# The second FFN product as seven Strassen products in turn, over slices of 512 tokens, with its operand sums made one stage earlier

## The chip, the core and the metric

One core of a Trainium2 chip runs the whole program. The metric is the device time of one execution in microseconds (us). The core has TensorE (PE, matrix products into PSUM; its weight loads stand as PEld), VectorE (DVE), ScalarE (ACT), GpSimd (POOL) and SyncE (SP, which here only issues DMAs). POOL and SP issue the DMAs; 16 DMA engines carry them.

## The reference, cut to what matters

```python
x = attention(q, k, v)                  # linear attention with decay, 4 x 768 tokens, 512 wide
x = ((x @ w1) * (x @ w2)) @ w3 @ w_out  # 3072 tokens, 512 -> 1024 -> 512
h = x @ w_in                            # first FFN product,  512 -> 2048
g = h * (1 / (1 + exp(-1.702 * h)))
out = g @ w_out2                        # second FFN product, 2048 -> 512
```

Everything is float32. The kernel writes each operand of a product as a high part plus a low part (dtype float32r) and adds three products: high times high, high times low, low times high. One such triple is `mm3` (L222 to L225 of the kernel before): three TensorE instructions.

## The kernel before, in words

The program has three parts in time. Attention and the weights' preparation come first, together with the MoE product (tiles `psm` and `acc`, 512 tokens to a matmul). Then comes the first FFN product (class `Expand`, called the second stage here), and then the second FFN product (`contract`, the third stage).

`Expand` runs over 4 slices `s` of 768 tokens and, in each, over 8 "quads" `j` of 256 features. A quad is one 2 x 2 block product by Strassen's scheme in Winograd's form: seven products P1, P5, P4 (of the quad before), P6, P2, P3, P7, each two `mm3` of 384 columns, so 42 matmuls. Sums of the seven give four quarters of h: two halves of the features by two halves of the 768 tokens. ACT copies partial results out of PSUM (L472) and applies the gate (L482), DVE adds (L510 `s1` after P2, L513 `u2` after P3, L519 `u3` after P7). The four gated quarters go to DRAM (`gd`, one tensor to a slice `s`) in two stores of 384 KB to a quad (L485), out of a pool of five tiles `g`. PSUM tiles turn over: `a` has three, `e` and `c` two each. The right operands of the next slice (`operands`, L405) are made on DVE in nine steps; the table `NEXT` puts eight of them after set products of quads 4 to 7, and the ninth falls into the next slice's first quad.

`contract` goes over 24 batches: 6 groups of 512 tokens by 4 groups of the contraction. A batch loads the gated values (`gr`, L565, 1 MB), makes four operand sums on DVE (L576), splits seven operands into parts (ACT L597, DVE L599), and runs all seven Strassen products for two steps of the contraction: 84 matmuls of 256 columns. Seven PSUM tiles `m` gather over four batches. At the end of a token group, DVE and POOL add the seven up (L669 to L686), and four stores write `out`. The weights' seven left operands are made in the first part (`seven`), written to DRAM by `store_parts` (`sp`, 16 tensors, one to a step of the contraction) and fetched with 1792 KB to a tile (L456) by POOL's queue into eight fixed slots `op0` to `op7`, which the second and the third stage share.

All engines run in the order in which the code is written (manual schedule). A tile's memory comes free when its last reader is done, and a new tile waits for all tiles whose bytes it covers. Each DMA that SP issues also waits for the one that used the same of its eight semaphores before.

Of the kernel before, what the change touches and what calls it, by code (L numbers as in the profile page):

```python
# [16 lines left out]
P = 128  # L17
# [24 lines left out]
def tile_kernel(  # L42
# [29 lines left out]
    gd = [dram.tile([P, NQ, 2, 2 * TS], F32, name=f"gd{i}", tag=f"gd{i}") for i in range(NS)]  # L72
    sp = [dram.tile([P, 2, 7 * 256], F32, name=f"sp{i}", tag=f"sp{i}") for i in range(2 * NQ)]
# [46 lines left out]
    def store_parts(i, m, hi, lo):  # L120
        at = slice(0, 3 * 256) if m == 0 else slice(3 * 256, 7 * 256)
        for n, x in enumerate((hi, lo)):
            nc.sync.dma_start(sp[i - WI][:, n, at], x.bitcast(F32))
# [337 lines left out]
    class Expand:  # L461
# [22 lines left out]
        def store(self, g, s, j, f):  # L484
            nc.sync.dma_start(gd[s][:, j, f], g.rearrange("p h t -> p (h t)"))  # L485

        def fourth(self):
            a, s, j, g = self.open
            self.product(a, "P4", s, j)
            self.gated(g[:, 0], a)  # L490
            self.store(g, s, j, 1)
            self.open = None

        def quad(self, s, j, step):
            a, e, c = (self.bank(x) for x in "aec")
            g = [self.p.tile([P, 2, TS], F32, tag="g", bufs=5, name="g") for _ in range(2)]
# [14 lines left out]
            self.gated(g[0][:, 0], s1)  # L511
# [10 lines left out]
            self.open = a, s, j, g[1]  # L522

        def run(self):
# [5 lines left out]
            for s in range(NS):  # L530

                for j in range(NQ):

                    def step(at):
                        nonlocal nxt
                        more = s + 1 < NS
                        if more and (j, at) == (2, 3):
                            nxt = operands(s + 1, self.py)
                            next(nxt)
                        elif more and (j, at) in NEXT:  # L540
                            next(nxt)
                        elif s and (j, at) == (0, 0):
                            next(nxt)
                        if not more and (j, at) in OPENING:
                            OPENING[j, at](self.py, self.pf)

# [5 lines left out]
    batches = [(i, b) for i in range(NB) for b in range(NQ // 2)]  # L552
    raws2, mid, ops = {}, {}, {}

    def load_g(n, pool, queue=nc.sync, **at):
        if n >= len(batches):
            return
        i, b = batches[n]
        raw = raws2[n] = pool.tile([P, 2, 2, TB], F32, name="gr", **at)
        at = 0  # L560
        while at < TB:
            s, t0 = divmod(i * TB + at, 2 * TS)
            m = min(TB - at, 2 * TS - t0)
            for k in range(2):
                queue.dma_start(  # L565
                    raw[:, k, :, at : at + m], gd[s][:, 2 * b + k, :, t0 : t0 + m]
                )
            at += m

    def sums(n, pool, **at):  # L570
        (b11, b12), (b21, b22) = (
            [raws2[n][:, :, f, h * TU : (h + 1) * TU] for h in range(2)] for f in range(2)
        )
        t = mid[n] = pool.tile([P, 4, 2, TU], F32, name="gt", **at)
        for x, (a, b) in enumerate(((b12, b11), (b22, t[:, 0]), (b22, b12), (b21, t[:, 1]))):
            nc.vector.tensor_tensor(t[:, x], a, b, ALU.subtract)  # L576

    def operand_tiles(n, pool, tags, **at):
        ops[n] = [
            pool.tile([P, 7, 2, TU], F32R, tag=tag, name=f"o{w}", **at)  # L580
            for w, tag in zip("hl", tags)
        ]

    def parts_of(n):
        r = raws2[n]
        yield 0, 1, r[:, :, 0, :TU]
        for h in range(2):
            yield 1 + h, 2 + h, r[:, :, 1, h * TU : (h + 1) * TU]
        yield 3, 7, mid[n]

    def splits(n):
        todo = [
            (*(o[:, a] if b - a == 1 else o[:, a:b] for o in ops[n]), x)
            for a, b, x in parts_of(n)
        ]
        for h, l, x in todo:
            nc.scalar.copy(h, x)  # L597
        for h, l, x in todo:
            nc.vector.tensor_tensor(l, x, h.bitcast(F32), ALU.subtract)  # L599

    def split_piece(a, b):
        if a < 3:
            x = list(parts_of(0))[a][2]
            h, l = (o[:, a] for o in ops[0])
        else:
            x = mid[0][:, a - 3 : b - 3]
            h, l = (o[:, a:b] for o in ops[0])
        nc.vector.tensor_copy(h, x)
        nc.vector.tensor_tensor(l, x, h.bitcast(F32), ALU.subtract)

    RIGHT = dict(P1=0, P2=1, P3=2, P5=3, P6=4, P7=5, P4=6)
    OPENING = {
        (0, 3): lambda p, pf: load_g(0, p, tag="raw"),
        (1, 3): lambda p, pf: sums(0, pf, tag=f"op{SLOT[0]}"),
        (3, 0): lambda p, pf: (
            operand_tiles(0, pf, [f"op{SLOT[x]}" for x in (1, 2)]),
            split_piece(0, 1),
        ),
        (3, 3): lambda p, pf: split_piece(1, 2),
        (4, 0): lambda p, pf: split_piece(2, 3),  # L620
        (4, 1): lambda p, pf: fetch_left(NQ, left_tile(pf, SLOT[3])),
        (4, 3): lambda p, pf: split_piece(3, 5),
        (5, 0): lambda p, pf: split_piece(5, 7),
        (5, 3): lambda p, pf: load_g(1, pf, tag=f"op{SLOT[0]}"),
        (5, 1): lambda p, pf: fetch_left(NQ + 1, left_tile(pf, SLOT[4])),
        (6, 1): lambda p, pf: fetch_left(NQ + 2, left_tile(pf, SLOT[5])),
        (7, 1): lambda p, pf: load_g(2, pf, tag=f"op{SLOT[6]}"),
    }

    def contract(p, pf, ps):  # L630

        def store(t, x, i, h):
            rows = out[x * 2 * P : (x + 1) * 2 * P].rearrange("(q p) t -> p q t", p=P)
            at = i * TB + h * TU
            nc.sync.dma_start(rows[:, :, at : at + TU], t)

        m = {}
        for n, (i, b) in enumerate(batches):
            if n == 1:
                for x in (1, 2):  # L640
                    fetch_left(NQ + 4 + x, left_tile(pf, SLOT[x]))
            hi, lo = ops[n]
            if b == 0:
                m = {
                    x: ps.tile([P, 2, TU], F32, tag=x, name="m") for x in RIGHT
                }
                c11, c12, c21, c22, s5, u3, u4 = (
                    p.tile([P, 2, TU], F32, tag=x, name=x)
                    for x in ("c11", "c12", "c21", "c22", "s5", "u3", "u4")
                )  # L650
            for k in range(2):
                j = 2 * b + k
                end = j == NQ - 1
                for name in ("P1", "P5", "P6", "P2", "P7", "P3", "P4"):
                    r = RIGHT[name]
                    for q in range(2):
                        mm3(
                            m[name][:, q],
                            *left_parts(NQ + j, name, q),
                            hi[:, r, k],  # L660
                            lo[:, r, k],
                            j == 0 and q == 0,
                            end,
                        )
                    if not end:
                        continue
                    ps_m = m[name]
                    if name == "P1":
                        nc.scalar.copy(c11, ps_m)  # L669
                    if name == "P5":  # L670
                        nc.scalar.copy(s5, ps_m)
                    if name == "P6":
                        nc.vector.tensor_tensor(c12, ps_m, c11, ALU.add)
                        nc.gpsimd.tensor_tensor(u4, c12, s5, ALU.add)
                    if name == "P2":
                        nc.vector.tensor_tensor(c11, ps_m, c11, ALU.add)
                        store(c11, 0, i, 0)
                    if name == "P7":
                        nc.vector.tensor_tensor(u3, ps_m, c12, ALU.add)
                        nc.gpsimd.tensor_tensor(c22, u3, s5, ALU.add)  # L680
                        store(c22, 1, i, 1)
                    if name == "P3":
                        nc.vector.tensor_tensor(c12, ps_m, u4, ALU.add)
                        store(c12, 0, i, 1)
                    if name == "P4":
                        nc.vector.tensor_tensor(c21, ps_m, u3, ALU.add)  # L686
                        store(c21, 1, i, 0)
# [299 lines left out]
```

## Time and profile before

| | |
|---|---|
| median of 3 runs | 1027.27 us (1027.13 to 1027.66) |
| the profiled execution | 1028.51 us, of which the span from first to last instruction is 1026.7 us |
| TensorE busy | 991.8 us (97%), 6688 matmuls |
| VectorE busy | 647.6 us (63%) |
| ScalarE busy | 441.8 us (43%) |
| mean granted TensorE clock | 0.993 of full speed |
| moved by DMA | 202.79 MB |

A matmul's busy time is longer than the distance to the next one, since matmuls overlap. What an instruction costs on TensorE is therefore read from the distance between starts in the timeline. "Idle before" is the time that an engine stood still ahead of an instruction, with what released it.

### The profile page before, as it was taken

What the parts mean: (1) busy time and instruction counts of PE and PEld (TensorE: products, weight loads), DVE (VectorE), ACT (ScalarE), POOL (GpSimd) and SP (SyncE); (2) the same over time, 40 slices, a digit from 0 to 9 for tenths busy, and PEclk for the clock granted to TensorE, in tenths of its full rate; (3) what the DMA queues carried; (4) which work ended last, traced back from release to release, by engine and by line L of the source; (5) the groups of instructions that cost most, each with busy time, mean ns of one, the idle gap of its engine ahead of it and who ended that gap; (6) DMA issues with size and microseconds to landing.
All of it is one profiled execution on the core that took longest, in us unless ns stands there. A gap on an engine that the chain in (4) does not pass through costs nothing.

```text
span 1026.7 us, 16851 instructions
## 1 busy us (share of the span) xinstructions
PE 991.8 (97%) x6688; PEld 900.1 (88%) x6688; DVE 647.6 (63%) x1048; ACT 441.8 (43%) x875; POOL 46.1 (4%) x65
## 2 busy tenths in 40 slices
PE   4879999999999999999999999999999999999997
PEld 3668777888888888888889999999999999999997
DVE  4877888856767777742442362634646588687782
ACT  4767544433434434322113455555455343433431
POOL 3110000000000000000001000000001011011011
PEclk9999999999999999999999999999999999999999
DMA  8999645436676666650137925233469854344331
GB/s 310 336 400 361 239 155 177 151 125 220 230 269 201 223 238 215 219 177 16 55 131 313 372 96 181 102 132 151 150 220 416 330 165 162 110 138 142 106 123 41
DMA packets 80159, 202.79 MB, mean 198 GB/s; under 512 B 6736, under 2 KB 33488, under 8 KB 75088
## 3 DMA queue, kind: packets, MB, share of 16 engines
q1 hardware_dynamic: 73888, 146.14, 40.8%
q0 software_dynamic: 6192, 55.58, 13.8%
q8 instruction: 52, 0.85, 0.3%
q14 instruction: 27, 0.22, 0.1%
HBM read 129.34 MB, written 72.35 MB: 196 GB/s over the span
## 4 chain that ended last, share of the span: by engine, by line
PE 87%; DMA 6%; DVE 4%; issue 1%; ACT 1%; POOL 0%; DVEq 0%; ACTq 0%; POOLq 0%
PE psm L225 8%; PE psm L224 8%; PE psm L223 8%; PE m L223 8%; PE m L225 8%; PE m L224 8%; PE acc L224 4%; PE acc L223 4%; PE acc L225 4%; DMA qkv<-in_qkv_dram 4%; PE a L223 4%; PE a L224 4%; PE a L225 4%; PE e L223 2%; PE e L224 2%; PE e L225 2%
## 5 line engine op out<-in xcount | busy, mean ns | idle before, releaser
L223 PE MATMUL m<-oh,op 128*128 128x256 f32 x672 | 188.2, 280 | 0.0
L225 PE MATMUL m<-oh,op 128*128 128x256 f32 x672 | 187.6, 279 | 0.0
L224 PE MATMUL m<-ol,op 128*128 128x256 f32 x672 | 187.6, 279 | 0.0
L225 PE MATMUL psm<-xh,wl 128*128 128x512 f32 x384 | 149.5, 389 | 1.2 <-DVE wl L118 1.2
L224 PE MATMUL psm<-xl,wh 128*128 128x512 f32 x384 | 149.4, 389 | 0.0
L223 PE MATMUL psm<-xh,wh 128*128 128x512 f32 x384 | 149.4, 389 | 0.0
L225 PEld LDWEIGHTS m<-oh,op 128*128 128x128 f32 x672 | 126.4, 188 | 0.0
L223 PEld LDWEIGHTS m<-oh,op 128*128 128x128 f32 x672 | 126.3, 188 | 0.0
L224 PEld LDWEIGHTS m<-ol,op 128*128 128x128 f32 x672 | 125.8, 187 | 0.0
L819 DVE TENSOR_TENSOR tmp<-tmp,psm 128x512 f32<-128x512 f32 x48 | 32.9, 686 | 103.9 <-PE psm L225 92.9
L225 PEld LDWEIGHTS psm<-xh,wl 128*128 128x128 f32 x384 | 72.1, 188 | 16.5 <-DVE wl L118 1.6
L223 PE MATMUL a<-yh,op 128*128 128x384 f32 x256 | 85.6, 335 | 0.6 <-ACT u L472 0.6
L597 ACT CAST oh<-gr 128x512 fp32r<-128x512 f32 x69 | 38.3, 618 | 111.1 <-issue 53.4
L225 PE MATMUL a<-yh,op 128*128 128x384 f32 x256 | 85.5, 334 | 0.0
L224 PE MATMUL a<-yl,op 128*128 128x384 f32 x256 | 85.5, 334 | 0.0
L223 PEld LDWEIGHTS psm<-xh,wh 128*128 128x128 f32 x384 | 72.1, 188 | 15.0
L224 PEld LDWEIGHTS psm<-xl,wh 128*128 128x128 f32 x384 | 72.1, 188 | 14.9
L800 ACT CAST hh<-tmp 128x512 fp32r<-128x512 f32 x48 | 29.8, 621 | 124.4 <-DVE tmp L819 124.4
L223 PE MATMUL acc<-hh,wh 128*128 128x512 f32 x192 | 74.7, 389 | 0.0
L224 PE MATMUL acc<-hl,wh 128*128 128x512 f32 x192 | 74.7, 389 | 0.0
L225 PE MATMUL acc<-hh,wl 128*128 128x512 f32 x192 | 74.7, 389 | 0.0
L510 DVE TENSOR_TENSOR s<-c,s 128x384 f32<-128x384 f32 x32 | 17.8, 557 | 83.5 <-PE c L225 79.3
(106 smaller groups left out, 1899.7 us busy)
## 6 DMA issues: line engine op xcount, KB each, us to landing
op<-sp POOLq DMA_DIRECT2D x16, 1792.0 KB, 10.6
gd<-g SPq DMA_DIRECT2D x64, 384.0 KB, 2.5
qkv<-in_qkv_dram POOLq DMA_DIRECT2D x23, 1024.0 KB, 8.2
raw<-in_w_dram SPq DMA_DIRECT2D x32, 512.0 KB, 4.7
gr<-gd SPq DMA_DIRECT2D x30, 512.0 KB, 4.7
raw<-in_wo_dram SPq DMA_DIRECT2D x24, 512.0 KB, 5.7
raw<-in_wi_dram SPq DMA_DIRECT2D x16, 512.0 KB, 4.6
sp<-wqh SPq DMA_DIRECT2D x16, 512.0 KB, 3.4
```

Source lines behind the costliest of these rows:

```text
L223: nc.tensor.matmul(ps, wh, xh, start=start, stop=False, skip_group_check=True)
L224: nc.tensor.matmul(ps, wh, xl, start=False, stop=False, skip_group_check=True)
L225: nc.tensor.matmul(ps, wl, xh, start=False, stop=stop, skip_group_check=True)
L510: nc.vector.tensor_tensor(s1, c, s1, ALU.add)
L597: nc.scalar.copy(h, x)
L800: nc.scalar.copy(hi, t)
L819: nc.vector.tensor_tensor(t, t, pb, ALU.mult)
```

## The change

The third stage no longer walks over the contraction with all seven products at once. It takes the seven products in turn (P1, P2, P6, P5, P3, P7, P4), and for each the three slices of 512 token columns: 21 turns. A Strassen half has 4 x 384 = 1536 token columns now (the halves are those of `Expand`), and a turn is the whole contraction of one product for 512 of them: 2 row blocks x 8 steps x 3 = 48 matmuls of 512 columns. The turn's right operand is loaded ready-summed from `gd` (two halves `l0`, `l1`, 1 MB each, three tiles each), ACT copies the high part (128x2048), DVE subtracts to leave the low part in place. The left operands of one product (all 8 steps, two parts) are loaded by product from `sw`. Results that later products need stay in SBUF (`u`, in slot 7 and later slots 2 and 3), and an output is stored as soon as its last product is there.

The operand sums move into `Expand`: four subtractions of 128x384 to a quad on DVE (one after L524, three in `fourth`). A quad now stores seven operands in one DMA of 1344 KB, and its tile `g` has two buffers where there were five tiles of two quarters. In the last slice, the loads and splits of turn 0 take the place of the first batch's. `store_parts` writes the last eight weight tiles to `sw` in pieces of 256 elements. POOL's DMA scratch is halved to 8192 bytes.

```diff
-    gd = [dram.tile([P, NQ, 2, 2 * TS], F32, name=f"gd{i}", tag=f"gd{i}") for i in range(NS)]
-    sp = [dram.tile([P, 2, 7 * 256], F32, name=f"sp{i}", tag=f"sp{i}") for i in range(2 * NQ)]
+    gd = [dram.tile([P, 7, NQ, TS], F32, name=f"gd{i}", tag=f"gd{i}") for i in range(NS)]
+    sp = [dram.tile([P, 2, 7 * 256], F32, name=f"sp{i}", tag=f"sp{i}") for i in range(NQ)]
+    sw = dram.tile([7, P, 2, NQ, 256], F32, name="sw", tag="sw")
...
         def fourth(self):
-            a, s, j, g = self.open
+            a, s, j, g, b12 = self.open
             self.product(a, "P4", s, j)
-            self.gated(g[:, 0], a)
-            self.store(g, s, j, 1)
+            self.gated(g[:, 1], a)
+            for x, y, z in ((5, g[:, 2], b12), (4, g[:, 2], g[:, 3]), (6, g[:, 1], g[:, 4])):
+                nc.vector.tensor_tensor(g[:, x], y, z, ALU.subtract)
+            nc.sync.dma_start(gd[s][:, :, j], g)
...
-            g = [self.p.tile([P, 2, TS], F32, tag="g", bufs=5, name="g") for _ in range(2)]
+            g = self.p.tile([P, 7, TS], F32, tag="g", bufs=2, name="g")
+            b12 = self.p.tile([P, TS], F32, tag="b", bufs=2, name="b12")
...
-            self.gated(g[0][:, 1], u2)
-            self.store(g[0], s, j, 0)
+            self.gated(b12, u2)
             nc.vector.tensor_tensor(u3, u3, s5, ALU.add)
-            self.late.append((g[1][:, 1], u3))
+            self.late.append((g[:, 2], u3))
+            nc.vector.tensor_tensor(g[:, 3], b12, g[:, 0], ALU.subtract)
...
+    turns = [(x, i) for x in ("P1", "P2", "P6", "P5", "P3", "P7", "P4") for i in range(3)]
...
+    def split_half(n, h, t, a=0, b=KH, copy=nc.scalar.copy):
+        high[n, h] = t
+        x = low[n, h][:, a:b]
+        copy(t[:, a:b], x.bitcast(F32))
+        nc.vector.tensor_tensor(x, x.bitcast(F32), t[:, a:b].bitcast(F32), ALU.subtract)
...
     def contract(p, pf, ps):
+        load_half(1, 1, half_tile(p, "l", 1, 3))
+        w_at = (4, 5), (0, 1)
+        u = [slot(pf, 7, [P, 3, 2, TB], F32)]
...
+        for n, (name, i) in enumerate(turns):
+            r = n // 3
+            load_turn(n + 2, p)
+            if i == 0 and n and r + 1 < 7 or n == 1:
+                nxt = turns[n + 3 - i][0]
+                for w in range(2):
+                    load_w(nxt, w, pf, w_at[(r + 1) % 2][w])
...
+            pq = [ps.tile([P, TB], F32, tag="m", bufs=6, name="m") for _ in range(2)]
+            for q in range(2):
+                for k in range(NQ):
+                    mm3(
+                        pq[q],
+                        *(t[:, k, q * P : (q + 1) * P] for t in ws[name]),
+                        high[n, k // KH][:, k % KH],
+                        low[n, k // KH][:, k % KH],
+                        k == 0,
+                        k == NQ - 1,
+                    )
+            split_turn(n + 1, p)
```

The change moves instructions at two places of which the prediction speaks. The first is VectorE where one slice of `Expand` passes into the next (from the last quad of the first slice on). `s` is the sum after P2, `u<-e` the one after P3, `u<-u,s` the one after P7; `yh`, `yl`, `yr` are the steps that make the next slice's operands. Before:

```order
L510 TENSOR_TENSOR s_5467<-c,s_5467 128x384
L513 TENSOR_TENSOR u_5496<-e,u_5496 128x384
L417 CAST yh<-yr 128x768
L418 TENSOR_TENSOR yl<-yr,yh 128x768
L422 TENSOR_TENSOR yr<-yr,yt 128x2x384
L519 TENSOR_TENSOR u_5528<-u_5528,s_5476 128x384
L417 CAST yh<-yr 128x768
L418 TENSOR_TENSOR yl<-yr,yh 128x768
L417 CAST yh<-yr 128x768
L418 TENSOR_TENSOR yl<-yr,yh 128x768
L510 TENSOR_TENSOR s_5548<-c,s_5548 128x384
```

The same place now; `g` and `b` are the gated quarters and their differences:

```order
L516 TENSOR_TENSOR s_5478<-c,s_5478 128x384
L519 TENSOR_TENSOR u_5510<-e,u_5510 128x384
L423 CAST yh<-yr 128x768
L424 TENSOR_TENSOR yl<-yr,yh 128x768
L428 TENSOR_TENSOR yr<-yr,yt 128x2x384
L524 TENSOR_TENSOR u_5542<-u_5542,s_5487 128x384
L526 TENSOR_TENSOR g<-b_5471,g 128x384
L423 CAST yh<-yr 128x768
L424 TENSOR_TENSOR yl<-yr,yh 128x768
L495 TENSOR_TENSOR g<-g,b_5471 128x384
L495 TENSOR_TENSOR g<-g 128x384 x2
L516 TENSOR_TENSOR s_5562<-c,s_5562 128x384
```

Between two sums after P2, four more subtractions stand (L526 once, L495 three times).

The second place is SP's queue where the second stage ends, each row with the semaphores that it waits for (SP's DMAs use the semaphores DMAHW0 to DMAHW7 in turn). Before, with the last store of `gd` and the loads around it:

```order
L485 DMA gd_83<-g 128x768 [waits DMAHW3_49,Activation_49]
L485 DMA gd_83<-g 128x768 [waits DMAHW4_49,Activation_49]
L485 DMA gd_83<-g 128x768 [waits DMAHW5_49,Activation_49]
L565 DMA gr<-gd_80 128x2x512 [waits DMAHW6_49,DMASW7_49,PE_49]
L565 DMA gr<-gd_80 128x2x512 [waits DMAHW7_49]
L485 DMA gd_83<-g 128x768 [waits DMAHW0_49,Activation_49]
L485 DMA gd_83<-g 128x768 [waits DMAHW1_49,Activation_49]
L565 DMA gr<-gd_80 128x2x256 [waits DMAHW2_49]
L565 DMA gr<-gd_80 128x2x256 [waits DMAHW3_49]
```

Now, from the last store of the last quad on; `l` with the lowest number is the second half of turn 1's operand:

```order
L496 DMA gd_83<-g 896x1x384 [waits DMAHW1_49,DVE_49]
L576 DMA l_7287<-gd_81 128x4x256 [waits DMAHW3_49,DMAHW5_49,DMAHW2_49,DMAHW1_49]
L576 DMA l_7287<-gd_82 128x4x256
L576 DMA l_7291<-gd_82 128x4x128 [waits DMAHW4_49]
L576 DMA l_7291<-gd_83 128x4x384
L576 DMA l_7294<-gd_82 128x4x128 [waits DMAHW6_49]
L576 DMA l_7294<-gd_83 128x4x384 [waits DMAHW7_49]
L576 DMA l_7355<-gd_80 128x4x384 [waits DMAHW0_49,PE_49]
```

The first load after the last store waits on the semaphore of that store (DMAHW1), because the tile `l_7287` covers bytes of the last `g`. Every later load of SP stands behind it.

## Rows read from the trace of the kernel before

**Rows 1.** The page's busy time of the engines over the span, with instruction counts.

```profile
PE 991.8 (97%) x6688; PEld 900.1 (88%) x6688; DVE 647.6 (63%) x1048; ACT 441.8 (43%) x875; POOL 46.1 (4%) x65
```

**Rows 2.** The page's chain that ended last, by engine.

```profile
PE 87%; DMA 6%; DVE 4%; issue 1%; ACT 1%; POOL 0%; DVEq 0%; ACTq 0%; POOLq 0%
```

**Rows 3.** Windows: stretch, its length, each engine's busy us (instructions), clock, DMA share, GB/s.

```profile
548.00:783.00 235.00, 233.95 (x1347) 233.19 (x1346) 104.13 (x166) 120.67 (x256) 5.13 (x9) 1.00 0.54 206
783.00:1021.00 238.00, 237.98 (x2019) 237.77 (x2017) 173.48 (x213) 88.25 (x106) 17.54 (x17) 1.00 0.46 161
1021.00:1027.00 6.00, 0.00 (x0) 0.00 (x0) 0.79 (x2) 0.00 (x0) 0.72 (x1) 0.67 0.46 156
```

**Rows 4.** Tile m: TensorE's first and last rows, ns min/median/max, first and last start.

```profile
L223 PE MATMUL m<-oh,op x672: 278/280/283, 783.2 to 1020.5; 128*128 128x256 f32 x168
...
L225 PE MATMUL m<-oh,op x672: 279/279/283, 783.4 to 1020.7; 128*128 128x256 f32 x168
```

**Rows 5.** TensorE timeline: two starts of 512-column matmuls, 21 apart (start, busy).

```profile
399.67 0.39 PE L223 MATMUL psm<-xh,wh 128*128 128x512 f32 x1
...
404.43 0.39 PE L223 MATMUL acc<-hh,wh 128*128 128x512 f32 x1
```

**Rows 6.** TensorE timeline at the second stage's end: first row to second, 41 starts of 384 columns.

```profile
774.03 0.33 PE L223 MATMUL a<-yh,op 128*128 128x384 f32 x1
...
781.14 0.34 PE L225 MATMUL a<-yh,op 128*128 128x384 f32 x1
782.05 0.45 PE L223 MATMUL a<-yh,op 128*128 128x384 f32 x1 [0.57 <-ACT u L472]
```

**Rows 7.** VectorE timeline between first and second slice of the second stage, idle in brackets.

```profile
592.75 0.56 DVE L519 TENSOR_TENSOR u<-u,s 128x384 f32<-128x384 f32 x1 [0.93 <-ACT u L472]
593.22 0.55 DVE L417 CAST yh<-yt 128x768 fp32r<-128x768 f32 x1
...
604.78 0.56 DVE L510 TENSOR_TENSOR s<-c,s 128x384 f32<-128x384 f32 x1 [0.21 <-PE c L225]
605.82 0.56 DVE L513 TENSOR_TENSOR u<-e,u 128x384 f32<-128x384 f32 x1 [0.48 <-PE e L225]
...
612.06 0.56 DVE L510 TENSOR_TENSOR s<-c,s 128x384 f32<-128x384 f32 x1
613.10 0.56 DVE L513 TENSOR_TENSOR u<-e,u 128x384 f32<-128x384 f32 x1 [0.48 <-PE e L225]
```

**Rows 8.** ScalarE timeline, the same place: the copy after P7 of the next slice's first quad.

```profile
614.07 0.48 ACT L472 COPY u<-a 128x384 f32<-128x384 f32 x1 [0.89 <-PE a L225]
```

**Rows 9.** Groups by line and shape: busy us, mean ns, idle before and its releaser.

```profile
L599 DVE TENSOR_TENSOR ol<-gt,oh 128x2048 fp32r<-128x2048 f32 x23 | 52.7, 2292 | 15.0 <-ACT oh L597 15.0
L597 ACT CAST oh<-gt 128x2048 fp32r<-128x2048 f32 x23 | 43.9, 1908 | 14.0 <-DVE gt L576 14.0
L472 ACT COPY u<-a 128x384 f32<-128x384 f32 x64 | 30.7, 480 | 46.9 <-PE a L225 46.9
L482 ACT ACTIVATE g<-s 128x384 f32<-128x384 f32 x32 | 16.9, 527 | 36.6 <-DVE s L510 36.6
L676 DVE TENSOR_TENSOR c<-m,c 128x512 f32<-128x512 f32 x6 | 4.2, 692 | 0.6
```

**Rows 10.** DMA queues: packets, MB, share; q0 of the whole span, q1 of 820 to 1027.

```profile
q0 software_dynamic: 6192, 55.58, 13.8%
...
q1 hardware_dynamic: 19584, 25.17, 37.3%
```

**Rows 11.** DMA issues, 560 to 735 and 820 to 1027: count, KB each, us to landing.

```profile
gd<-g SPq DMA_DIRECT2D x48, 384.0 KB, 2.3
yr<-yd SPq DMA_DIRECT2D x3, 1024.0 KB, 8.2
...
gr<-gd SPq DMA_DIRECT2D x24, 512.0 KB, 4.4
```

**Rows 12.** Tile gd's landings over the run, min/median/max.

```profile
DMA to landing us min/median/max: 2.3/3.9/29.6
```

More of the change, by code (lines that the diff above doesn't have):

```diff
@@ L551, in tile_kernel @@
     NEXT = (4, 3), (5, 1), (5, 3), (6, 3), (7, 0), (7, 1), (7, 2), (7, 3)
[L552 to L559, printed above, removed]
+    RIGHT = dict(P1=0, P2=1, P3=2, P5=3, P6=4, P7=5, P4=6)
+    turns = [(x, i) for x in ("P1", "P2", "P6", "P5", "P3", "P7", "P4") for i in range(3)]
@@ L578, in operand_tiles @@
[L578 to L627, printed above, removed]
@@ new lines, in split_turn, with load_w, opening_split, run @@
+    def split_turn(n, p):
+        if n < len(turns):
+            for h in range(2):
+                split_half(n, h, half_tile(p, "h", h, 2))
+    def load_w(name, w, pf, at):
+        t = slot(pf, at, [P, NQ, 256])
+        ws.setdefault(name, []).append(t)
+        nc.gpsimd.dma_start(t.bitcast(F32), sw[PART[name], :, w])
+    def opening_split(h, a):
+        def run(pf):
+            if a == 0:
+                high[0, h] = slot(pf, 2 + h, [P, KH, TB])
+            split_half(0, h, high[0, h], a, a + 1)
+        return run
@@ L628, in tile_kernel @@
     }
     def contract(p, pf, ps):
[L632 to L687, printed above, removed]
-                if k == 0 and n + 1 < len(batches):
-                    sums(n + 1, p, tag="t")
-                    if n == 0:
-                        load_g(3, p, nc.gpsimd, tag="raw", bufs=2)
-                        fetch_left(NQ + 3, left_tile(pf, SLOT[7]))
-                    operand_tiles(n + 1, p, ("oh", "ol"), bufs=2)
-                    splits(n + 1)
-                    if n == 0:
-                        p.tile([P, 48], F32, name="gap")
-                    if n:
-                        load_g(n + 3, p, tag="raw", bufs=2)
-                    if n < 2:
-                        fetch_left(NQ + (4, 7)[n], left_tile(pf, SLOT[(0, 6)[n]]))
@@ new lines, in contract, with add, store @@
+        load_half(1, 1, half_tile(p, "l", 1, 3))
+        w_at = (4, 5), (0, 1)
+        u = [slot(pf, 7, [P, 3, 2, TB], F32)]
+        def add(out, x, y):
+            nc.vector.tensor_tensor(out, x, y, ALU.add)
+        def store(x, h, i, q, value):
+            t = p.tile([P, TB], F32, tag="o", bufs=4, name="c")
+            add(t, *value)
+            at = 0
+            while at < TB:
+                s, t0 = divmod(i * TB + at, TS)
+                m = min(TB - at, TS - t0)
+                to = s * 2 * TS + h * TS + t0
+                rows = slice((2 * x + q) * P, (2 * x + q + 1) * P)
+                nc.sync.dma_start(out[rows, to : to + m], t[:, at : at + m])
+                at += m
@@ new lines, in contract @@
+        for n, (name, i) in enumerate(turns):
[5 more added lines that the diff above has]
+                    load_w(nxt, w, pf, w_at[(r + 1) % 2][w])
+            if name == "P5" and i == 0:
+                u += [slot(pf, x, [P, 3, 2, TB], F32) for x in (2, 3)]
+            pq = [ps.tile([P, TB], F32, tag="m", bufs=6, name="m") for _ in range(2)]
[8 more added lines that the diff above has]
+                        k == NQ - 1,
+                    )
+            split_turn(n + 1, p)
+            for q, m in enumerate(pq):
+                ua, p5, u4 = (t[:, i, q] for t in (u * 3)[:3])
+                if name == "P1":
+                    nc.scalar.copy(ua, m)
+                if name == "P2":
+                    store(0, 0, i, q, (m, ua))
+                if name == "P6":
+                    add(ua, m, ua)
+                if name == "P5":
+                    nc.scalar.copy(p5, m)
+                    add(u4, ua, p5)
+                if name == "P3":
+                    store(0, 1, i, q, (m, u4))
+                if name == "P7":
+                    add(ua, m, ua)
+                    store(1, 1, i, q, (ua, p5))
+                if name == "P4":
+                    store(1, 0, i, q, (m, ua))
@@ L968 @@
     given.update(zip(("cmask", "cy", "cstep", "cv"), _constants()))
[L970 removed]
+    nc = _bacc.Bacc(
+        "TRN2", target_bir_lowering=False, num_devices=1, dynamic_dma_scratch_size=8192
+    )
     arrays, args = {}, []
```

59 lines of the change are left out of this document (39 added, 20 removed).

## The prediction

> **What bounds the kernel now.** I read the busy time first, then the chain of waits, then the stages. TensorE is busy for 97% of the span [rows 1], and the chain that ended last is TensorE for 87% [rows 2]: almost every microsecond that the reader wants back has to come out of matmuls. The windows [rows 3] show both stages that the change touches with TensorE at 234 of 235 us and 238 of 238 us at full clock, so neither waits for anything worth naming. The one stall is 0.57 us ahead of the second stage's last P4 [rows 6]. The change has therefore one way to gain, fewer or shorter matmuls in the third stage, and many ways to lose, waits where there are none.
>
> **What the third stage's matmuls cost.** They are read by the distance of starts. Before there are 3 x 672 = 2016 of 256 columns, and from 783.2 to 1020.7 us [rows 4] lie 2015 distances: 237.5 / 2015 = 117.9 ns each, 237.6 us in all. The changed stage has 21 turns x 48 = 1008 matmuls of 512 columns, which the kernel already runs in the MoE product: 21 starts from 399.67 to 404.43 us are 226.7 ns each [rows 5]. That was with DMAs and both other engines at work beside it, as it will be. 1008 x 226.7 = 228.5 us. The columns are the same, 516,096 either way; what goes is 2 x 117.9 - 226.7 = 9.1 ns for each pair that becomes one. Gain: 9.1 us. The second stage keeps its 384 columns at (781.14 - 774.03) / 41 = 173.4 ns [rows 6], 42 x 173.4 ns = 7.28 us to a quad.
>
> The Trainium skill, on the page TensorE: Matmul & The Clock Gate, section Back-to-back issue gap, gives the distance at full clock as columns / 2.4 plus 2.5 ns. By that the halved count would be worth 1008 x 2.5 ns = 2.5 us and not 9.1. The rows speak against it: 226.7 and 117.9 ns stand where it says 215.8 and 109.2. It is kept as a rival below.
>
> **What the sums cost in the second stage.** Four subtractions of 128x384 come to each quad on VectorE. One such, out of SBUF, occupies it for 593.22 - 592.75 = 0.47 us [rows 7], so 1.9 us of the 7.28. In most quads VectorE waits for TensorE, and they are free there. Where one slice passes into the next they are not: quads 6 to 8 carry the operand steps as well, and from 600 us until the sum after P2 of the next slice's first quad, at 612.06, VectorE stood idle for only 0.21 + 0.48 us [rows 7]. Eight subtractions, 3.8 us, now go into that stretch, so this sum comes 3.1 us late. Behind it queue ScalarE's gate, then its copy of P7's bank, and for that copy TensorE's P4 waits. ScalarE has 0.89 us in hand before the copy, which lasts 0.48 from 614.07 [rows 8], and P4 is due two products (12 x 173.4 ns = 2.1 us) after P7, so 1.6 us more: 2.5 in all. 3.1 - 2.5 is 0.6 us; the third subtraction waits for the gate after P4 and adds some tenths. I take 0.9 us at each of the three passages, 2.7 us; the ends are 0 (the queue absorbs it) and 2 each, 6 us.
>
> **The store of seven operands.** It must land before its tile, one of two, is written again: issued about 4.2 us into the next quad (P1, P5, P4, a gate, a subtraction), needed 5.9 us into the one after (P2, its sum), 9.0 us later. The queue rows give packet prices: q0's 13.8% of 16 x 1026.7 us over 6192 packets is 366 ns for 8976 B, q1's 37.3% of 16 x 207 us over 19584 is 63.1 ns for 1285 B [rows 10]; the line through both is 12.5 ns + 0.0394 ns/B. A store of 384 KB, 128 packets of 3072 B, is 1.07 us of that on 16 engines and lands after 2.3 [rows 11]. The new one is 896 packets of 1536 B, 73 ns each: 4.1 us, landing after 5.3. It is hidden with 3.7 us in hand. If it isn't, that is a rival.
>
> **The passage into the third stage.** SP's first load after the last store, the second half of turn 1's operand, waits for that store to land, and all of SP's loads queue behind it. From the last P4's end: gate 0.53 and subtraction 0.5, store 5.3, so 6.4 us. The load is 1 MB in packets of 1024 B (52.8 ns): 3.4 us and some 1.4 to land, 11.2 us; by the loads of 512 KB at 4.4 us, each in a burst of up to four [rows 11], it could be 6 us instead of 4.8. Then ScalarE's cast 1.9 and VectorE's subtraction 2.3 [rows 9]: 15.4. TensorE has turn 0, 48 x 226.7 ns = 10.9 us, and 13 matmuls of turn 1, until 13.8. It waits 1.6 us. Bounds 0 and 4 us.
>
> **Steady turns.** A turn lasts 10.9 us. ScalarE has two casts, 3.8 us, and VectorE two subtractions and at most four sums of 0.69, 7.4 us [rows 9]: hidden. DMA is the closest: 2048 packets of on average 1024 B are 6.8 us on 16 engines, a third of 256 weight packets of 8192 B (335 ns) is 1.8, stores of 512 packets in four turns of seven are 1.0. 9.5 of 10.9 us, 88%, and a load has two turns to land. I cost it at nothing; without that cover it is the second rival.
>
> **The rest at nothing.** The smaller pieces to `sw` add packets, not waits, on a queue that TensorE doesn't wait for at that time. The smaller scratch holds the same DMAs. POOL's sums vanish, but TensorE was past them. The end after the last matmul, 1020.7 to 1026.7 us [rows 3, 4], is again one sum out of PSUM and a store. Each plus or minus 0.5 us.
>
> **Sum.** -9.1 + 2.7 + 1.6 = -4.8 us. The profiled execution, 1028.51 us, becomes 1023.7; against the median of 1027.27, 1.2 us lower, it is 1022.5 us.
>
> **Rivals.**
> - The waits don't come: the queues absorb both. For it speaks that ScalarE and VectorE wait for TensorE in nearly every quad; against it, the stretch of rows 7. Time 1027.3 - 9.1 + 0.5 = 1018.7 us.
> - The waits are at their upper ends, 6 + 4 us: 1027.3 - 9.1 + 10 = 1028.2 us, no change. Rows 7 and the landings of up to 29.6 us in the present passage [rows 12] speak for it; the latter are those of a crowd of weight loads that the change takes away.
> - DMA sets the pace of the third stage. The 88% above is a price from mixed sizes; loads of 512 KB, 1.5 us by that price, took 4.4 us to land. If a turn's packets need 11.3 us instead of 9.5, 20 turns lose 0.43 us each: 8.7 us, 1031 us.
> - The store lands too late, the slower side. Beyond 9.0 us, each pair of quads is as long as the store's excess, 16 pairs in the stage. At 10.5 us it costs 24 us: 1047 us. It decides from 9.0 us on; loads of 1 MB and more beside it (8.2 us to land [rows 11]) come once in a slice and five times in the last one, which speaks for it; the 5.3 us of a store alone speak against it.
> - The distance at 512 columns isn't that of rows 5 in the new stage, and only the page's 2.5 us are saved: 1027.3 - 2.5 + 4.3 = 1029.1 us.
>
> **How the numbers follow.** Forecast 50% (1020 to 1025 us), no waits 20%, upper ends 13%, DMA's pace 8%, late store 6%, small saving 3%. Differences under 0.2%, 2.05 us, can't be told from none in this kernel, so faster means below 1025.2: the first two, 70%. Within it lie the upper ends, most of the small saving and a little of the rest, 16%. Slower, above 1029.3, 14%. The range from 1018 to 1031 leaves out the late store, half of DMA's pace and a little below.
>
> **What would show it.** Right: matmuls `m` 226.7 ns apart, one wait of 1 to 2 us ahead of the 13th or 14th matmul of turn 1 put down to VectorE's `l`, three waits of about 1 us ahead of P4 put down to ScalarE's copy `u`, `gd` stores landing in 5 to 6 us. Wrong: waits of ScalarE's gate for the landing of `gd` in many quads (late store), waits for `l` or `h` in turns from the third on (DMA's pace), or a distance of `m` above 230 ns.

## The result, and the profile after

The changed kernel takes 1037.58 us (median of 5 runs, 1034.6 to 1040.05), the kernel before 1027.47 beside it: the ratio is 1.0098, 95% interval 1.0072 to 1.0123. It is slower by 1%, where 0.5% faster was forecast, and outside the range. The profiled run took 1040.05 us, the longest of the five and 11.5 more than the profiled run before; what follows is read from it.

The page first: TensorE's busy time fell by 4.3 us, and its share of the chain from 87 to 80%, with DMA and VectorE in its place [rows 1, 2].

```profile
PE 987.5 (95%) x5680; PEld 854.2 (82%) x5680; DVE 649.4 (63%) x1038; ACT 436.9 (42%) x831; POOL 32.1 (3%) x57
...
PE 80%; DMA 8%; DVE 7%; issue 2%; ACT 2%; POOL 0%; SPq 0%; DVEq 0%; ACTq 0%; POOLq 0%
```

Then the windows of the two stages, columns as in [rows 3]:

```profile
548.00:794.00 246.00, 237.09 (x1345) 235.45 (x1345) 160.94 (x285) 120.97 (x264) 3.16 (x6) 0.99 0.71 254
794.00:1034.00 240.00, 230.38 (x1008) 189.88 (x1006) 118.33 (x84) 82.73 (x53) 6.28 (x12) 0.98 0.77 259
```

Both stages have TensorE idle for some 9 us, and a clock under 1.00, where before it was idle for 1.1 us in both together, at a clock of 1.00. By first and last starts, the second stage went from 234.6 to 246.1 us, and the third from 237.5 to 240.2. The piece behind the last matmul is 1.6 us shorter, what comes ahead of the second stage 0.9 us. 11.5 + 2.7 - 1.6 - 0.9 and -0.1 around the span are the 11.5 (with rounding).

What TensorE waited for in the two stages (total us, times, longest):

```profile
PE a L229 <- ACT u L478: 8.9, 5, 5.3
PE m L229 <- ACT h L590: 8.1, 1, 8.1
PE m L230 <- DVE l L591: 1.5, 1, 1.5
```

They are seven waits. The timeline has each (start, duration, in brackets the idle time before it and its releaser). They are the start of the second stage; the first of three equal passages between slices; the last P4; turn 1 of the third stage:

```profile
570.38 0.34 PE L231 MATMUL e<-yh,op 128*128 128x384 f32 x1
576.03 0.69 PE L229 MATMUL a<-yh,op 128*128 128x384 f32 x1 [5.31 <-ACT u L478]
...
623.41 0.44 PE L229 MATMUL a<-yh,op 128*128 128x384 f32 x1 [0.69 <-ACT u L478]
...
792.57 0.45 PE L229 MATMUL a<-yh,op 128*128 128x384 f32 x1 [1.53 <-ACT u L478]
...
807.15 0.39 PE L231 MATMUL m<-h,o 128*128 128x512 f32 x1
815.63 0.80 PE L229 MATMUL m<-h,o 128*128 128x512 f32 x1 [8.09 <-ACT h L590]
817.95 0.79 PE L230 MATMUL m<-l,o 128*128 128x512 f32 x1 [1.53 <-DVE l L591]
```

Two starts of `m` 21 apart, and the tile's rows (ns min/median/max, first and last start), answer to [rows 4, 5]:

```profile
849.85 0.39 PE L229 MATMUL m<-h,o 128*128 128x512 f32 x1
...
854.61 0.39 PE L229 MATMUL m<-h,o 128*128 128x512 f32 x1
```

```profile
L229 PE MATMUL m<-o,o x16: 389/389/397, 793.7 to 804.0; 128*128 128x512 f32 x16
...
L231 PE MATMUL m<-h,o x320: 387/389/629, 805.1 to 1033.9; 128*128 128x512 f32 x160
```

4.76 / 21 = 226.7 ns, as forecast. VectorE at the first passage answers to [rows 7]: three subtractions of the quad that ends, a cast of the operand step (its subtraction follows), then the sum after P2, with no idle time ahead of any:

```profile
618.82 0.55 DVE L495 TENSOR_TENSOR g<-g,b 128x384 f32<-128x384 f32 x1
619.29 1.21 DVE L495 TENSOR_TENSOR g<-g 128x384 f32<-128x384 f32 x2
620.42 0.56 DVE L423 CAST yh<-yr 128x768 fp32r<-128x768 f32 x1
...
621.89 0.55 DVE L516 TENSOR_TENSOR s<-c,s 128x384 f32<-128x384 f32 x1
```

The passages and the last P4 are what the prediction spoke of, and the passages have its size. The other two places are the loss. At each, ScalarE's timeline names a DMA:

```profile
575.09 0.52 ACT L488 ACTIVATE g<-s 128x384 f32<-128x384 f32 x1 [9.00 <-DMA gd<-g]
...
813.68 1.90 ACT L590 CAST h<-l 128x2048 fp32r<-128x2048 f32 x1 [12.74 <-DMA l<-gd]
```

The first waits until the first quad's store has landed, because its tile, one of two, is to be written again. SP's rows give both transfers' issue (SPq is a DMA that SP issues; x2 means that the view draws two together):

```profile
558.34 7.83 SPq L496 DMA_DIRECT2D gd<-g  x2
...
795.42 0.52 SPq L496 DMA_DIRECT2D gd<-g  x1
802.37 19.23 SPq L576 DMA_DIRECT2D l<-gd  x12
```

The store issued at 558.34 took 16.7 us to land, and the next one 17.0, the longest of all (the expectations below give the first one the 17.0), while the median of the 17 between 608 and 735 us is 5.7, near the 5.3 that was priced. The rows that answer to [rows 12] and [rows 11] (the loads of `l` are those from 830 us on):

```profile
DMA to landing us min/median/max: 2.8/6.3/17.0
```

```profile
gd<-g SPq DMA_DIRECT2D x17, 1344.0 KB, 5.7
...
l<-gd SPq DMA_DIRECT2D x20, 512.0 KB, 5.5
```

The load of turn 1's second half was issued at 802.37, when the last store had landed, and ScalarE had it at 813.68, 11.3 us later instead of 4.8. Who holds them up is seen in the DMA queues of 552 to 560 us (packets, MB, share of 16 engines):

```profile
q0 software_dynamic: 239, 2.98, 87.2%
q1 hardware_dynamic: 239, 0.42, 13.8%
```

The two queues send equally many packets. POOL's are up to 14336 B long (the second stage's weights), SP's 2048 B and below, so SP gets 0.42 MB in 8 us, 52 GB/s of 426. The Trainium skill, page DMA: Bandwidth & Descriptors, section Queues, rings and completion order, has each DMA engine go round the queue rows packet by packet; the 239 and 239 agree. The page's typical packet holds several descriptors; no run here shows how many one of the profile's holds. At the second place, while POOL's third-stage weights are under way, it is the same (805 to 807 us):

```profile
q0 software_dynamic: 82, 0.66, 81.3%
q1 hardware_dynamic: 86, 0.09, 12.4%
```

Last, the clock behind the two long waits:

```profile
576.00:581.00 5.00, 4.97 (x16) 4.97 (x17) 2.61 (x5) 2.53 (x6) 0.00 (x0) 0.50 1.07 431
...
811.00:821.00 10.00, 3.84 (x8) 2.75 (x9) 4.58 (x2) 6.11 (x5) 0.00 (x0) 0.50 1.07 354
```

The granted clock, 1.00 ahead of the waits (2.4 GHz), falls to 0.50 (1.2 GHz) before they end and stays there through some 6 us of work at the first place and 3 at the second. That work took nearly twice as long: starts of 384 columns are 0.32 us apart instead of 0.17, of 512 columns 0.43 instead of 0.23.

### The profile page after: what moved, and what is told of

Same layout as the page of the kernel before. It is cut to its first block, busy times and chain, and to the rows that moved or that the text cites. A ratio compares the mean times of both kernels' runs of the same rounds, so it can differ in the third digit from the quotient of the medians.

```text
span 1038.3 us, 14825 instructions
## 1 busy us (share of the span) xinstructions
PE 987.5 (95%) x5680; PEld 854.2 (82%) x5680; DVE 649.4 (63%) x1038; ACT 436.9 (42%) x831; POOL 32.1 (3%) x57
## 4 chain that ended last, share of the span: by engine, by line
PE 80%; DMA 8%; DVE 7%; issue 2%; ACT 2%; POOL 0%; SPq 0%; DVEq 0%; ACTq 0%; POOLq 0%
PE psm L231 8%; PE psm L230 8%; PE psm L229 8%; PE m L230 7%; PE m L231 7%; PE m L229 7%; PE acc L230 4%; PE acc L229 4%; PE acc L231 4%; DMA gd<-g 3%; DMA qkv<-in_qkv_dram 3%; PE a L229 3%; PE a L231 3%; PE a L230 3%; PE e L229 2%
## 5 line engine op out<-in xcount | busy, mean ns | idle before, releaser
L229 PE MATMUL m<-h,o 128*128 128x512 f32 x320 | 125.5, 392 | 8.1 <-ACT h L590 8.1
L231 PE MATMUL m<-h,o 128*128 128x512 f32 x320 | 125.0, 391 | 0.0
L230 PE MATMUL m<-l,o 128*128 128x512 f32 x312 | 122.2, 392 | 1.5 <-DVE l L591 1.5
L590 ACT CAST h<-l 128x2048 fp32r<-128x2048 f32 x39 | 74.1, 1912 | 102.0 <-DMA l<-gd 58.4
L591 DVE TENSOR_TENSOR l<-l,h 128x2048 fp32r<-128x2048 f32 x39 | 88.0, 2286 | 35.6 <-ACT h L590 35.5
L229 PE MATMUL a<-yh,op 128*128 128x384 f32 x256 | 87.0, 340 | 8.9 <-ACT u L478 8.9
L231 PE MATMUL a<-yh,op 128*128 128x384 f32 x256 | 86.4, 337 | 0.0
L229 PEld LDWEIGHTS m<-h,o 128*128 128x128 f32 x320 | 60.5, 189 | 21.2 <-ACT h L590 8.5
L231 PEld LDWEIGHTS m<-h,o 128*128 128x128 f32 x320 | 60.5, 189 | 12.4
L230 PEld LDWEIGHTS m<-l,o 128*128 128x128 f32 x312 | 59.0, 189 | 14.3 <-DVE l L591 2.0
```

Source lines behind the costliest of these rows:

```text
L229: nc.tensor.matmul(ps, wh, xh, start=start, stop=False, skip_group_check=True)
L230: nc.tensor.matmul(ps, wh, xl, start=False, stop=False, skip_group_check=True)
L231: nc.tensor.matmul(ps, wl, xh, start=False, stop=stop, skip_group_check=True)
L590: copy(t[:, a:b], x.bitcast(F32))
L591: nc.vector.tensor_tensor(x, x.bitcast(F32), t[:, a:b].bitcast(F32), ALU.subtract)
```

## The experiments

All are edits of the changed kernel, 1037.6 us. Times are medians with their lowest and highest; the kernel before, beside them, had 1027.9, 1028.2 and 1028.4. The stages are compared by their lengths in the traces, since runs of one kernel differ by up to 6 us, of one by 7 and of one by 11; why they do stays open. A trace is that of one run, so a stage's length is less sure than a single wait in it.

**Turn 1's load off the last store.**

```diff
+        p.tile([P, TB], F32, tag="o", bufs=4, name="c")
         load_half(1, 1, half_tile(p, "l", 1, 3))
```

> One edit at the passage into the third stage: the pool of that stage hands out its output tile first, so that turn 1's second operand half no longer lies on the last quad's g tile and its load needn't wait for that tile's store. Theory A (the load was late because it waited for the store, 795.4 to 802.4 us, and then met POOL's P2 weight loads): the load is issued at about 795.5 us, lands before 807 us, TensorE's wait in turn 1 falls from 9.6 to between 0 and 2 us and the half clock behind it goes too: 8 to 11 us less than the changed kernel's 1037.6, 1026.5 to 1029.5 us. Rival B (the load is slow wherever it starts, behind 1.3 MB of store on the same queue): it lands at 811 us or later, the wait stays above 6 us and the time above 1034 us. The wait of 5.3 us near 570 us stays in both.

Measured: 1034.83 us (1032.17 to 1036.94), third stage 235.1 us instead of 240.2.

```profile
797.35 0.52 SPq L496 DMA_DIRECT2D gd<-g  x1
797.92 24.37 SPq L576 DMA_DIRECT2D l<-gd  x12
...
809.37 1.90 ACT L590 CAST h<-l 128x2048 fp32r<-128x2048 f32 x1 [7.08 <-DMA l<-gd]
```

The load no longer waits, and is 11.4 us under way all the same, now behind 1.3 MB of store. TensorE's waits fell from 9.6 to 1.85 + 1.83 us, and the clock still fell to 0.50 behind them. Theory A is right on the wait for the store, wrong in that this alone would settle it: the load lands between A's 807 and B's 811 us, and the time is on B's side.

**The third stage's weights on SP's queue.**

```diff
-        nc.gpsimd.dma_start(t.bitcast(F32), sw[PART[name], :, w])
+        nc.sync.dma_start(t.bitcast(F32), sw[PART[name], :, w])
```

> One edit: the weights of the third stage (1 MB each, packets of 8192 B) are loaded on SP's queue, behind the operand loads in program order, instead of POOL's. The load of turn 1's second half still waits for the last store. Theory A (two queues share the engines packet by packet, so that POOL's large packets starve SP's small ones): the load issued at 802.4 us lands in 5 to 6 us instead of 11.3; TensorE's wait falls from 9.6 to 3 to 5 us; the wait ahead of the last P4, 1.53 us, falls to 0.6 or so; 5 to 9 us less than 1037.6: 1029 to 1033 us. Rival B (1 MB in packets of 1024 B takes 11 us by itself, or the store is what counts): wait stays 9 us or more, 1036 to 1039 us.

Measured: 1037.0 us (1034.31 to 1039.16), third stage 236.3 us.

```profile
801.09 9.82 SPq L576 DMA_DIRECT2D l<-gd  x10
...
806.60 1.90 ACT L590 CAST h<-l 128x2048 fp32r<-128x2048 f32 x1 [8.10 <-DMA l<-gd]
```

Issue to cast is 5.5 us instead of 11.3, the load's price without POOL's packets beside it; TensorE waits 2.98 + 1.82 us, and the last P4 0.57 as before the change. The mechanism holds. The median is above what was expected: the two stages are 5.4 us shorter in the traces, but that is the shortest of its four runs against the longest of the changed kernel's five. The medians are 0.6 us apart, so a gain in time isn't shown by this run.

**The weights of quads 3 to 7 behind the stores.** POOL issues three at once; SP gets one behind each of the first stores:

```diff
-            for n in range(NQ):
-                fetch_left(n, homes[SLOT[n]])
+            for n in range(3):
+                fetch_left(n, homes[SLOT[n]], nc.gpsimd)
...
+                        if s == 0 and at == 0 and 0 < j < 6:
+                            fetch_left(j + 2, homes[SLOT[j + 2]], nc.sync)
```

> One edit at the start of the second stage: of the eight weight loads of 1792 KB that POOL issues at once, three stay there, and those of quads 3 to 7 go on SP's queue, one behind each of the first stores. Theory A (the store of the first quad, 17.0 us to land, is starved by POOL's packets of 14336 B): it lands in 6 to 8 us, the wait of 5.31 us near 570 us goes, and with it the stretch at half clock behind it (2.9 us): about 8 us less than 1037.6, 1028.5 to 1031 us. Rival B (the first store itself, or ScalarE, is slow there for another reason): the wait stays above 3 us. Rival C (the weights of quads 3 to 7 now come late): new waits of TensorE for op ahead of P1 of quads 3 to 7, and no gain.

Measured: 1044.6 us (1043.18 to 1044.69). Rival C:

```profile
PE a L229 <- DMA op<-sp: 6.7, 4, 4.5
PE a L229 <- ACT u L478: 2.1, 3, 0.7
```

The wait for the store went (what is left of `u` up to 790 us are the three passages), and four waits for weights came. POOL had been issuing those of quads 0 to 2 early (509.8, 510.7 and 542.7 us in the changed kernel) and that of quad 3 at 545.2; the last was in nobody's way and was delayed for nothing. Mended:

```diff
+            for n in range(4):
+                fetch_left(n, homes[SLOT[n]], nc.gpsimd)
...
+                        if s == 0 and at == 0 and 0 < j < 5:
+                            fetch_left(j + 3, homes[SLOT[j + 3]], nc.sync)
```

> The third edit of the first call, mended: there the weights of quad 3 were late because they too had been put behind a store. Now POOL issues those of quads 0 to 3 as before and those of quads 4 to 7 go on SP's queue, one behind each of the first four stores. Theory A (the first store is starved by the weights of quads 4 to 6): it lands in 6 to 8 us, no wait near 570 us, no half clock there, and the weights are in time: second stage 238 to 239.5 us instead of 246.1, the time 7 us less than 1037.6: 1029.5 to 1031.5 us. Rival B (the weights on SP's queue are late again, since 1.8 MB behind 1.3 MB of store and the next slice's operand take too long): waits for op ahead of quads 4 to 7 of more than 2 us in all.

Measured: 1036.21 us (1035.47 to 1037.44), some 5 us above what was expected; second stage 241.6 us instead of 246.1. The first store lands after 7.2 us. No wait near 570 us, none for weights; a smaller one two quads on, where the store of quad 2 is behind two loads:

```profile
587.75 0.44 PE L229 MATMUL a<-yh,op 128*128 128x384 f32 x1 [1.98 <-ACT u L478]
```

The clock fell behind it too (0.50 from 590 to 592 us). Theory A on the store; the stage is 2 to 3.6 us longer than expected: SP's queue now has some 12 us of transfers in one quad of 7.3 by the prices of the prediction.

**Packets of POOL made smaller.** The same loads on POOL in four pieces each:

```diff
-        nc.gpsimd.dma_start(t.rearrange("p a b c -> p a (b c)").bitcast(F32), sp[n])
+        for a in range(2):
+            for b in ((0, 3), (3, 7)):
+                nc.gpsimd.dma_start(
+                    t[:, a, slice(*b)].rearrange("p b c -> p (b c)").bitcast(F32),
+                    sp[n][:, a, b[0] * 256 : b[1] * 256],
+                )
```

> One edit: each of the eight weight loads of the second stage on POOL's queue is issued in four pieces, with packets of 3072 and 4096 B instead of 14336 B; the same bytes, the same queue, nearly the same times of issue. Theory A (the DMA engines take a packet from each queue in turn, so a queue's share goes by the size of its packets): SP's queue gets two to three times the share it had, the first quad's store lands in 7 to 11 us instead of 17.0, and TensorE's wait near 570 us falls from 5.31 us to between 0 and 1.5; with the half clock gone, 5 to 8 us less than 1037.6: 1029.5 to 1032.5 us. Rival B (the bytes of both queues together take that long, whatever the packets): the store lands in 15 us or more, wait above 4 us, time 1036 to 1039 us.

Measured: 1041.11 us (1040.02 to 1041.93), wait 6.82 us, landing 18.2. The queues from 552 to 560 us, and from 565 to 577:

```profile
q0 software_dynamic: 570, 2.30, 69.8%
q1 hardware_dynamic: 543, 1.01, 32.7%
...
q0 software_dynamic: 886, 3.63, 73.6%
q1 hardware_dynamic: 884, 1.33, 29.6%
```

Packets still go one for one, and SP's queue has 111 to 126 GB/s instead of 52: the share goes by packet size. But the forecast made from it was wrong: landing and wait are where rival B had them, and the time is above both ranges. By the traces, the four stores of `yd` ahead of the store landed sooner, and that set free the last weight load, which waits for the memory they read (issued at 572.3 us in the changed kernel, in pieces from 565.5 to 572.2 here). So POOL's packets went on without a break until 580 us, where in the changed kernel they stopped from 570 to 576 and the store had the engines to itself. Sharing better didn't help the store here; fewer bytes beside it did, in the run before this one.

**The sums on POOL around the passages.**

```diff
+        def engine(self, j):
+            return nc.gpsimd if j in (0, 6, 7) else nc.vector
...
-                nc.vector.tensor_tensor(g[:, x], y, z, ALU.subtract)
+                self.engine(j).tensor_tensor(g[:, x], y, z, ALU.subtract)
```

> One edit: the four subtractions of a quad are made by POOL in the quads around the passage between slices (quads 0, 6 and 7 of each slice) and by VectorE in the others. Theory A (the passages wait because VectorE has four subtractions a quad more): the three waits of TensorE near 622, 682 and 741 us fall from 0.69 to about 0.1 us each, 2 to 3 us less in all: 1034.5 to 1036 us, if nothing else changes. Rival B (the passages wait for the landing of stores and of the next slice's operand beside them): the three waits stay. POOL took 1.30 us for a sum of 128x512 in the kernel before, so some 1 us each: the store of these quads goes out 1.5 to 2 us later, and where it was late already, in the first and last quads of the stage, waits can grow by up to 2 us.

Measured: 1048.3 us (1045.3 to 1051.95), 12 us above Theory A's range. Two things were overlooked. VectorE's operand step becomes longer while POOL has a sum under way (0.96 us elsewhere):

```profile
628.21 3.01 POOL L498 TENSOR_TENSOR g<-g 128x384 f32<-128x384 f32 x2
...
628.70 1.65 DVE L424 TENSOR_TENSOR yl<-yr,yh 128x768 fp32r<-128x768 f32 x1
```

The Trainium skill, page GPSIMD Engine Reference, section Specifications, names such a contention with VectorE's instructions of two SBUF inputs; the 1.65 us agree. And in quad 0 the sums are queued on POOL behind its last weight load, which waits until 572 us: the first store went out later, and TensorE waited 12.81 us near 571 us. The passages became longer (0.69 + 0.49). It tells nothing on what makes them.

**The sums behind, at the passages.** VectorE's work stays; in the first quad of a slice the three subtractions and the store (now `sums`) come behind the sums after P2 and P3:

```diff
-            if self.open:
-                self.fourth()
+            todo = self.fourth() if self.open else None
+            if todo and j:
+                self.sums(*todo)
...
+            if todo and not j:
+                self.sums(*todo)
             step(2)
```

> One edit at the passages between slices: in the first quad of a slice the three subtractions that follow P4, and the store of the operands, are issued behind the sums after P2 and P3 instead of ahead of them; VectorE's work stays the same. Theory A (TensorE waits at the passage because these 1.5 us of subtractions stand in VectorE's queue ahead of the operand step and of the sum after P2, on which ScalarE's gate and then the copy u hang): the sum after P2 comes 1.5 us earlier, the three waits of 0.69 us go, 2 to 2.7 us less in the second stage (246.1 us from its first matmul to the third stage's): 243.5 to 244.2 us. Rival B (VectorE and POOL or the DMAs beside it set the passage): the waits stay. The run of the POOL sums has shown that moving the sums to POOL doesn't settle it, since VectorE's operand steps became longer (0.96 to 1.65 us) while POOL worked. Total time 1034 to 1037 us by A, 1036 to 1039 us by B.

Measured: 1035.09 us (1029.78 to 1040.39, 10 runs), second stage 243.7 us, 2.4 less. TensorE is busy without a gap where the changed kernel has 59.31 of 60 us (columns: stretch, length, TensorE, clock, DMA share, GB/s):

```profile
608.00:668.00 60.00, 60.00 (x348) 1.00 0.63 222
668.00:728.00 60.00, 60.00 (x347) 1.00 0.61 215
```

Theory A: the order of VectorE's queue makes the passages, and the subtractions cost nothing elsewhere.

**Turn 1 in halves,** with the first two edits:

```diff
+            at = [(q, k) for q in range(2) for k in range(NQ)]
+            if n == 1:
+                at.sort(key=lambda x: (x[1] // KH, x[0], x[1]))
```

> Three edits at the passage into the third stage together: the two of the first call (the load of turn 1's second half off the last g tile, the weights on SP's queue), and turn 1 goes through the first half of its operand for both halves of the output rows before it turns to the second, which moves TensorE's need of the second half from 13.8 us after the stage's start to 16.3. Alone the two left waits of 3.7 and 4.8 us of the 9.6. Theory A (what is left is the chain of store, load behind it, cast 1.9 us and subtraction 2.3 us): the load lands about 12.5 us after the stage's start, hi is there at 14.5 and lo at 16.8, so TensorE waits 0 to 0.6 us in turn 1, the granted clock stays 1.0, and the third stage takes 229 to 231 us from its first to its last matmul instead of 240.2: 1028 to 1030 us. Rival B (the half clock comes back whatever the wait, or the load lands later): above 233 us.

Measured: 1028.15 us (1025.19 to 1029.37), the level of the kernel before (ratio 0.9992, 0.9981 to 1.0003). The third stage takes 229.3 us, with one wait of 0.70 us and the clock at 1.00. Theory A, to the microsecond.

**Together.**

> All edits that helped, together: the load of turn 1's second half off the last g tile, the third stage's weights on SP's queue, turn 1's order by halves, the weights of quads 4 to 7 behind the first four stores, the three subtractions and the store behind the sums at the passages. If the gains add: the second stage 241.6 us as with the weights behind the stores, less 2.4 for the passages and 0.7 for the last P4, 238.5 us; the third stage 229.3 us as with turn 1 in halves; with 548.3 us ahead, 4.5 us behind the last matmul and 1.8 us around the span: 1022 to 1023 us, faster than the kernel before (1028.2) by 0.5%. If they don't add (the DMAs that were moved meet others, and the wait near 585 us of 2.0 us with its half clock grows): 1026 to 1029 us.

Measured: 1023.86 us (1020.94 to 1025.25), ratio 0.9951 (0.9937 to 0.9966); stages of 238.1 and 229.3 us, against 238.5 and 229.3 expected. The gains add; the median is 0.9 us above the range given, the traced run below it. What is left are waits of 1.71 us near 585 us (the clock stays 1.00 behind it), 0.49, 0.29, 0.57 and 0.67 us. The last kernel spreads the weight loads better: POOL issues five at once, SP the other three:

```diff
+                        if s == at == 0 and j in (1, 3, 4):
+                            n = {1: 5, 3: 6, 4: 7}[j]
+                            fetch_left(n, homes[SLOT[n]], nc.sync)
```

> As the run with all edits, but with the weight loads spread otherwise: POOL issues those of quads 0 to 4 at once, and SP those of quads 5, 6 and 7 behind the stores of quads 0, 2 and 3, so that the next slice's operand (1.5 MB) doesn't meet one of them. Theory A (the 2.0 us wait near 585 us comes of 11.8 us of DMA in one quad of 7.3): no wait above 1 us in the first slice, the clock stays 1.0, second stage 235.5 to 237 us, time 1020 to 1021.5 us. Rival B (the first store is starved again, now by the weights of quad 4 on POOL): a wait of 1 to 4 us near 570 us, 1022 to 1026 us.

Measured: 1018.27 us (1016.16 to 1022.04), ratio to the kernel before 0.9904, 0.9886 to 0.9921: faster than both. Stages of 233.8 and 228.4 us in the traced run, the shortest of the six. TensorE's waits from 547 to 1012 us are one, that of [rows 6]:

```profile
PE a L229 <- ACT u L478: 0.6, 1, 0.6
```

```profile
548.00:781.00 233.00, 232.43 (x1341) 232.11 (x1340) 160.12 (x284) 120.24 (x263) 0.40 (x1) 1.00 0.73 266
781.00:1010.00 229.00, 228.99 (x1011) 189.18 (x1009) 118.29 (x85) 83.06 (x54) 0.00 (x0) 1.00 0.80 272
```

Theory A holds, by more than it said: the second stage came out 1.7 us below its lower end.

## Why the prediction was wrong

- **The gain, 9.1 us: right.** Without waits the third stage takes 228.4 us in the last kernel, where 1008 x 226.7 ns = 228.5 was forecast, against 237.5. The rival of 2.5 us is dead, and so is DMA's pace: behind turn 1 nothing waits, neither in the changed kernel nor in the last.
- **The passages, 2.7 us: right.** The sum after P2 comes 3.7 us behind the start of P2's last matmul, where it came 0.4 behind: 3.2 us late, 3.1 forecast. Starts at 622.38, 623.41 and 623.69 us instead of 0.17 apart are 0.96 us, three times 2.9, and the queue order on VectorE makes them, as shown by putting the subtractions behind.
- **"It is hidden with 3.7 us in hand": wrong, and the first cause.** The store's price was right (5.7 us in steady quads), its company was not looked at. The 9.0 us of cover were held against a store alone. At the stage's start four weight loads of 1792 KB, which the kernel before issues there too, leave SP's queue 52 GB/s. The store took 16.7 us. The trace of the kernel before had shown it: from 552 to 560 us its queues share packets in the same way, and its first two stores, of 384 KB, took 18.3 and 16.8 us to land; [rows 11] begin at 560 us, behind both. With five tiles of `g` ScalarE waited for the first of them all the same, and TensorE stood still for 0.48 us at 575.26, a second stall that the prediction missed. In the changed kernel the late store cost 5.3 us of waiting and, at half clock, about 3 more. The late store was among the rivals, but for every second quad, at 6%, and its crowd was placed in the slice's loads. The kernel before:

```profile
q0 software_dynamic: 232, 2.95, 86.3%
q1 hardware_dynamic: 236, 0.45, 14.6%
...
574.32 0.53 ACT L482 ACTIVATE g<-u 128x384 f32<-128x384 f32 x1 [3.13 <-DMA gd<-g]
```

- **"It waits 1.6 us" in turn 1: mis-sized, 9.6.** The chain was right, store, load, cast, subtraction; two of its terms were not. The last store landed after 7 us, not 5.3; the load took 11.3, not 4.8, because POOL's next weights start at 802.2, when turn 0's slots come free. The bound of 4 us was worked out from loads on the same queue; the landing of 29.6 us [rows 12] was put aside as the doing of a crowd that goes, when another stands in its place.
- **The clock: no term at all.** Each long wait was costed at its length. Behind 5.3 us came some 6 us of work at 1.2 GHz, behind turn 1's waits some more.
- **The last P4, at nothing: 1 us.** 1.53 us instead of 0.57, from a store late beside weights on POOL; on SP's queue it is 0.57 again.

The sum as it came out for the profiled run: -9.1 (matmuls), +2.9 (passages), +8.3 (start of the second stage with its half clock), +1.0 (last P4), +11.8 (turn 1 with its half clock), -0.8 (the kernel before's stall at 575.26, which went), -2.6 (the ends): 11.5. All the loss is in waits and what follows them, and the last kernel gets all of it back in its traced run.

## What to carry to other kernels

A store that becomes something that is waited for (fewer buffers) has to be held against everything that is on the DMA engines at each place where it is issued, at the stage's starts and ends above all, and against loads that had nobody waiting until then. Price the queue with the small packets by what the other queue leaves it, and put loads that aren't urgent behind the urgent store on one queue rather than beside it on another. A wait of several microseconds on TensorE costs more than its length.

## What the runs showed of the hardware

- Two DMA queues with work share by packets, one for one: 239 and 239 at up to 14336 against 2048 B and less (52 GB/s for the small), 82 and 86 at up to 8192 against 1024 B, 886 and 884 at 3072 to 4096 against 1536 B (111 GB/s).
- The granted clock fell to 0.50 in a wait of 5.31 us, about 1.5 us behind one of 1.98, and in two of 1.85 and 1.83 with one matmul between, and stayed there for some 3 to 6 us of work; it stayed at 1.00 behind waits of 1.71, of 2.00 and of 0.7 us and below. The wait's length alone doesn't decide.
- A VectorE subtraction of 128x768 took 1.65 us instead of 0.96, a cast 1.37 instead of 0.55, while POOL made sums.
